# Two segments inverted as one pair at the start, and the feed-forward one step behind the chain from chunk 1 on

## The chip, the cores and the metric

One core of one Trainium2 chip runs the whole program. The metric is the device time of one execution in microseconds, median of several. The engines are TensorE (PE; PEld is its weight load), VectorE (DVE), ScalarE (ACT), GpSimd (POOL) and the queue of SyncE (SP) that issues most transfers.

## What is computed

A delta-rule attention, token by token, and a gated MLP on its output (batch 4, 8 heads, 768 tokens, head width 48; model width 384, 1024 hidden):

```python
for t in range(S):                       # k_n = k / (|k| + 1e-6)
    y[:, :, t] = q_t @ state
    v_old = k_n_t @ state
    state = state + beta_t * outer(k_n_t, v_t - v_old)
x = y as [B, S, 384]
h = gelu_tanh(x @ w_in); u, v = halves of h
v_n = layer_norm(v) * g_ln
out = x + (u * (w_sg @ v_n + b_sg)) @ w_out
```

## The kernel before

The recurrence runs in 12 chunks of 64 tokens; two chunks are a segment (six segments). Two batches lie side by side on the partitions, and 16 columns j hold heads and halves. For each chunk:

- `gram` makes k'k and k'q on TensorE and ScalarE copies them to GM (8 buffers). `kgram` makes k'k alone, `qgram` k'q alone; `dense` makes a whole gram without a chain beside it. The keys and queries come by `kload` (KD, two buffers, for grams) and `qload` (KQ, for the chain); `vload` and `tload` bring v and k by token.
- `gstore` writes the 32x32 diagonal blocks to DRAM (gd), four transfers a chunk; `zload` reads them back as lanes (tile zl), one 32x32 matrix per partition, one transfer a segment.
- `lanes` inverts them on VectorE: a copy of the diagonals (L323), two triangles cut by GpSimd (L325, `triu`), a reciprocal root (L176 to L184), scaling (L352), then for each row an outer product and an addition (L368, L375), and a last scaling (L396). It handles one segment (m = 1) or a pair (m = 2) in the same instructions. `zstore` writes the result to DRAM (zd, L421), `zfetch` reads it per chunk into Z and zk (L430, L435); `turned` transposes zk (L444), `corner_a` and `corner_b` build the off-diagonal block of the 64x64 inverse on TensorE.
- `above` masks k'q (L257), `vprep` scales v (L483).
- `chain` has the serial steps old0, own0, state0, old1, own1, state1: products with the state S, an addition into v on VectorE after old0 and old1 (L510, "the first and second addition"), copies by ScalarE (L532, L545, L560). A step of the chain is dealt alternately with a piece of a later chunk's gram.

The feed-forward of a chunk (`Ffn`) has a turn (transposes, L664, and the split into xh and xl, L665, L668), four `gate` groups and two `values` groups (L642 to L644, L678) with their gelu and moments (L684, L690). Its weights w_in come as 64-bit words and are decoded on VectorE in six pieces of three units each (`decode_win`, L584 to L602, ScalarE's copy at L594); the first three pieces serve the gates, the others the values. The load of piece k + 2 is issued on GpSimd's queue when piece k is done.

The order is written out by hand. Ahead of the loop stand the first inversion and grams; then the loop goes through `TURNS`, pairs (chunk of the chain, chunk of the feed-forward). Before, these are (0, none), (1, none), (2, none), (3, 0), (none, 1), (none, 2), (4, 3), (5, 4), ... (11, 10), (none, 11). A turn without a chain ends with a `zfetch` and both corners of the next chunk; `zfetch` for chunk 4 is issued twice. VectorE's background work (lanes, decoding) stands in the list `bg` with a cost for each unit; every step of a turn gives `tick` its planned cost times SHARE[turn] / length, and as many units are issued as the credit pays for. `lanes_done` and `until` issue the rest at once. All engines run their instructions in the order of issue.

Groups before: segments 0 and 1 alone, (2, 3) and (4, 5) as pairs. The lanes of (2, 3) are queued at the end of chunk 1's turn, together with their zload, those of (4, 5) in the turn before chunk 4.

From chunk 8 on (`c == NCH - 4`) the weights of the spatial part are brought in beside the turns; after the last turn comes the spatial part.

Of the kernel before, what the change touches and what calls it, by code (L numbers as in the profile page):

```python
# [26 lines left out]
NP = 16  # L27
# [13 lines left out]
N_GRAMS = 6  # L41
N_EARLY = 5
N_ROWS = (0, 6, 1)
N_COLS = (0, 5, 1)
GROUPS = ((0,), (1,), (2, 3), (4, 5))
# [3 lines left out]
TURNS = ((0, None), (1, None), (2, None), (3, 0), (None, 1), (None, 2),  # L49
         *((c, c - 1) for c in range(4, NCH)), (None, NCH - 1))  # L50
TURNED = {0: 0, 1: 1, 3: 2, 4: 3, **{c + 2: c for c in range(4, NCH)}}
# [3 lines left out]
def delta_rule_gmlp_kernel(  # L55
# [134 lines left out]
    gdt, zsrc, ztile, zds, zks, ns, nvs, ztks, j1s = {}, {}, {}, {}, {}, {}, {}, {}, {}  # L190
# [22 lines left out]
    def kgram(c):  # L213
        def phase(e):
            st = {}

            def step(h):
                if h == 0:
                    st["ps"] = bank().rearrange("p (j t) -> p j t", t=T)
                for sd in range(2):  # L220
                    kk = KD[c % N_2][OWN[sd], 0, 8 * e + h]
                    mm(st["ps"][TOK[sd ^ e], h], kk, kk)

            def done():
                nc.scalar.copy(out=GM[c % N_M][:, 8 * e:8 * e + 8, 0], in_=st["ps"])

            return step, done

        return phase(0), phase(1)
# [79 lines left out]
    def lanes(g):  # L309
# [56 lines left out]
        def outer(i, r0, r1, at):  # L366
            w = 31 - i
            tv.tensor_tensor(  # L368
                out=st["tmp"][:, at:at + m * (r1 - r0) * w].rearrange("p (m r t) -> p m r t", m=m, t=w),
                in0=z[:, :, r0:r1, i:i + 1].broadcast_to([P, m, r1 - r0, w]),  # L370
                in1=z[:, :, i:i + 1, i + 1:32].broadcast_to([P, m, r1 - r0, w]), op=ALU.mult)

        def add(i, r0, r1, at):
            w = 31 - i
            tv.tensor_tensor(  # L375
                out=z[:, :, r0:r1, i + 1:32], in0=z[:, :, r0:r1, i + 1:32],
                in1=st["tmp"][:, at:at + m * (r1 - r0) * w].rearrange("p (m r t) -> p m r t", m=m, t=w),
                op=ALU.add)

        us = lambda n: (0.13 if m == 1 else 0.17) + n / 960  # L380
        ops = [(f, us(32 * m)) for f in first] + [(scale, m * us(1024))]
        for i in range(1, 31):
            w = 31 - i
            if i <= N_ROWS[m]:
                ops += [(lambda a=a, r=r, i=i: row(a, r, i), us(w)) for r in range(i) for a in range(m)]
            elif w <= N_COLS[m]:
                ops += [(lambda a=a, t=t, i=i: column(a, t, i), us(i)) for t in range(i + 1, 32) for a in range(m)]
            else:
                parts = [(0, i // 2, 0), (i // 2, i, 256)] if m == 1 else [(0, i, 0)]
                ops += [(lambda i=i, p=p, f=f: f(i, *p), us(m * (p[1] - p[0]) * w)) for f in (outer, add) for p in parts]  # L390
# [3 lines left out]
        def last():  # L394
            for a in range(m):
                tv.tensor_tensor(  # L396
                    out=z[:, a], in0=z[:, a], in1=nb[:, a].unsqueeze(1).broadcast_to([P, 32, 32]), op=ALU.mult)
            ztile[g] = z

        return ops + [(lambda: tv.memset(dg, 1.0), us(0)), (last, m * us(1024)), (lambda: zstore(g), 0.0)]  # L400
# [15 lines left out]
    def zstore(g):  # L416

        z = ztile[g]
        for a, s in enumerate(GROUPS[g]):
            zd = dram.tile([2, 2, 2, NP, 32, 32], F32, name="zd", bufs=4)  # L420
            nc.sync.dma_start(out=zd.rearrange("a b c j s t -> (a b c j) s t"), in_=z[:, a])  # L421
            zds[s] = zd
# [383 lines left out]
    for c, q in ((0, nc.sync), (1, nc.scalar)):  # L806
        load(q, KD[c][:, 0], kqT[c, 0:2])
# [9 lines left out]
    for c in range(2):  # L817
# [5 lines left out]
    zload(0)  # L823
    for _ in range(N_EARLY):
# [8 lines left out]
    kload(2)  # L833
    kload(3)
    vload(0)
    tload(0)
    qload(0)
    for c in (2, 3):
        dense(c)
        gstore(c, (nc.sync,))  # L840
    zload(1)
    qload(1)
    kload(4)
    kload(5)
    for op, _ in first:
        op()
    norms(0)
    for c in range(2):
        q0, q1 = qgram(c)
        deal([q0], [q1])  # L850
    zfetch(0, nc.scalar)
    zfetch(1, nc.sync)
    bg += lanes(1) + win
    above(0)
    vprep(0)
    tick(5.0)
    for c in (4, 5):
        dense(c)
    kload(6)
    win_load(2, nc.sync)  # L860
    for c in (4, 5):
        gstore(c, (nc.sync,))
# [4 lines left out]
    tick(6.0)  # L867
# [18 lines left out]
    SHARE = (20.0, 20.0, 19.0, 20.0, 16.0, 16.0, 13.0, 13.0, 13.0, 13.0, 11.0, 11.0)  # L886
    units, turns = [], {}
    ffn = None
    for at, (c, f) in enumerate(TURNS):
# [55 lines left out]
        kload(new + 1)  # L945
        does("old0")
        if n is not None and n // 2 in zds and n not in zks:
            zfetch(n, nc.sync)
        if n is not None:
            above(n)  # L950
        if f == 0:
            until(lambda: not win_left)
# [5 lines left out]
        if c:  # L958
            qload(c + 1)
        feeds("values", 4)  # L960
        does("old1")
        unit()
        feeds("values", 4)
        does("own1")
        if c is not None:
# [19 lines left out]

        if ch:
# [5 lines left out]
        if at in TURNED:  # L992
            turns[TURNED[at]] = following = Ffn(TURNED[at])
# [20 lines left out]
        if c == 1:  # L1014
            zload(2)
            zload(3)
            bg.extend(lanes(2))
        if n == 4:
            zload(4)
            zload(5)  # L1020
            bg.extend(lanes(3))
# [123 lines left out]
```

## Time and profile before

| what | us |
|---|---|
| runs | 541.64, 538.8, 541.56 |
| median | 541.56 |
| span of the profiled execution | 538.2 |
| TensorE busy | 441.4 (82%) |
| VectorE busy | 346.6 (64%) |
| ScalarE busy | 171.8 (32%) |
| GpSimd busy | 74.9 (14%) |

The page gives the profiled execution's span, not the time around it; the median of the runs lies 3.4 us above the span. The chain of work that ended last is 61% TensorE, 17% VectorE and 7% transfers. Shares of the whole span mix stages with different limits, so the rows below are read by stretches: about 0 to 62 us is the front, 62 to 284 the turns of chunks 0 to 7, 284 to 370 the turns of chunks 8 to 11, the rest the spatial part.

### The profile page before, as it was taken

To read this page: it belongs to the slowest core of one execution; us is meant where nothing else is said; L and a number is where in the kernel's file an instruction comes from. 1 tells how busy PE (TensorE), PEld (TensorE's weight loads), DVE (VectorE), ACT (ScalarE), POOL (GpSimd) and SP (SyncE) were. 2 spreads that over 40 slices of the span, in tenths; PEclk is the share of its full clock that TensorE was granted. 3 is DMA by queue.
4 is the path that set the end of the run, shared out by engine and by line. 5 is a ranking of instruction groups with operands and counts; after the bars stand their busy time and mean duration, and the time that the engine had idled before them with its cause. 6 is when DMAs were issued, how large, how long until landed. Compare 5 with 4: busy or idle time off the path is not lost.

```text
span 538.2 us, 17698 instructions
## 1 busy us (share of the span) xinstructions
PE 441.4 (82%) x7691; PEld 395.2 (73%) x7691; DVE 346.6 (64%) x858; ACT 171.8 (32%) x383; POOL 74.9 (14%) x87
## 2 busy tenths in 40 slices
PE   4316785570889949898989896999998999999997
PEld 2316475470778748687777775878898999999997
DVE  3999999648997229689913359643599636623332
ACT  3222333230423522333533533444534213211110
POOL 2100002102201004010010110000024223222130
PEclk9555756555599969899999998899999999999999
DMA  7987858965538796645955868265857753344204
GB/s 181 278 199 195 179 156 211 248 174 126 156 95 237 218 206 165 195 117 165 314 146 155 277 154 250 65 202 163 246 161 187 214 166 104 103 147 147 74 16 132
DMA packets 111965, 93.18 MB, mean 173 GB/s; under 512 B 74768, under 2 KB 88016, under 8 KB 111888
## 3 DMA queue, kind: packets, MB, share of 16 engines
q1 hardware_dynamic: 101504, 68.23, 45.3%
q0 software_dynamic: 6032, 22.28, 15.0%
q10 hardware_dynamic: 4352, 1.54, 1.2%
q8 instruction: 60, 0.98, 0.8%
q14 instruction: 17, 0.14, 0.1%
HBM read 63.69 MB, written 28.34 MB: 171 GB/s over the span
## 4 chain that ended last, share of the span: by engine, by line
PE 61%; DVE 17%; DMA 7%; issue 7%; ACT 4%; SPq 4%; ACTq 1%; DVEq 0%
PE ps L81 19%; PE ps L642 12%; PE ps L644 11%; PE ps L643 11%; PE ps L678 8%; DVE ztmp L368 3%; DVE zl L375 3%; DMA kd<-kqT 2%; DMA vraw<-vD 2%; PE ps L664 1%; DMA gd<-gm 1%; DMA zl<-gd 1%; SPq L752 1%; ACT gm L295 1%; DVE zl L357 1%
## 5 line engine op out<-in xcount | busy, mean ns | idle before, releaser
L81 PEld LDWEIGHTS ps<-s,kq 48*64 48x64 f32 x1408 | 55.8, 159 | 21.3 <-issue 14.8
L81 PE MATMUL ps<-s,kq 48*64 48x48 f32 x1408 | 63.1, 245 | 9.7 <-issue 8.3
L785 POOL TENSOR_TENSOR ga<-ga,uT 128x384 f32<-128x384 f32 x32 | 36.3, 1140 | 165.8 <-DVE ga L782 120.9
L81 PE MATMUL ps<-kd 48*64 48x128 f32 (+1 forms) x768 | 40.2, 337 | 19.4 <-DMA kd<-kqT 17.4
L81 PE MATMUL ps<-v,z 64*64 64x48 f32 x768 | 33.7, 244 | 23.2 <-DVE v L510 13.8
L81 PEld LDWEIGHTS ps<-kd 48*64 48x64 f32 x768 | 33.8, 177 | 22.9 <-DMA kd<-kqT 15.3
L81 PEld LDWEIGHTS ps<-v,z 64*64 64x64 f32 x768 | 30.4, 159 | 24.5 <-DVE v L510 14.4
L368 DVE TENSOR_TENSOR ztmp<-zl 128x120 f32<-128x120 f32 (+25 forms) x132 | 45.9, 372 | 2.2
L375 DVE TENSOR_TENSOR zl<-zl,ztmp 128x120 f32<-128x120 f32 (+25 forms) x132 | 45.7, 370 | 1.6
L642 PE MATMUL ps<-xh,winh 128*128 128x256 f32 x144 | 45.7, 317 | 0.9 <-DVE xl L668 0.9
L643 PE MATMUL ps<-xl,winh 128*128 128x256 f32 x144 | 42.1, 293 | 0.4 <-DVE xl L668 0.3
L644 PE MATMUL ps<-xh,winl 128*128 128x256 f32 x144 | 41.8, 290 | 0.0
L647 ACT CAST gh<-ga 128x384 fp32r<-128x384 f32 x32 | 16.3, 511 | 77.3 <-POOL ga L785 63.3
L81 PE MATMUL ps<-u,gm 64*64 64x48 f32 x768 | 34.1, 245 | 2.6 <-ACT u L532 1.9
L648 DVE TENSOR_TENSOR gl<-ga,gh 128x384 fp32r<-128x384 f32 x32 | 18.1, 565 | 26.8 <-ACT gh L647 26.7
L532 ACT COPY u<-ps 128x384 f32<-128x384 f32 x24 | 11.5, 479 | 70.6 <-PE ps L81 70.6
L644 PE MATMUL ps<-wouth,gl 128*128 128x384 f32 x96 | 32.3, 340 | 1.5 <-DVE gl L648 1.5
L81 PEld LDWEIGHTS ps<-u,gm 64*64 64x64 f32 x768 | 30.2, 159 | 4.4 <-ACT u L532 2.4
L642 PE MATMUL ps<-wsgh,vnh 128*128 128x384 f32 x96 | 32.7, 340 | 0.7 <-ACT vnh L755 0.6
L81 PE MATMUL ps<-u,kt 64*48 64x48 f32 x704 | 27.3, 234 | 6.4 <-issue 4.6
L643 PE MATMUL ps<-wsgl,winh 128*128 128x384 f32 x96 | 32.5, 339 | 0.0
L642 PE MATMUL ps<-wsgh,winh 128*128 128x384 f32 x96 | 32.5, 339 | 0.0
(127 smaller groups left out, 1097.2 us busy)
## 6 DMA issues: line engine op xcount, KB each, us to landing
kq<-kqT POOLq DMA_DIRECT2D x10, 896.0 KB, 6.8
uD<-ut SPq DMA_DIRECT2D x12, 512.0 KB, 5.2
vD<-vg SPq DMA_DIRECT2D x24, 256.0 KB, 4.0
vraw<-vD SPq DMA_DIRECT2D x48, 128.0 KB, 3.1
uT<-uD SPq DMA_DIRECT2D x8, 768.0 KB, 5.4
kd<-kqT SPq DMA_DIRECT2D x6, 896.0 KB, 8.3
xD<-x SPq DMA_DIRECT2D x12, 384.0 KB, 6.9
x<-xD SPq DMA_DIRECT2D x48, 96.0 KB, 2.8
```

The lines of the kernel that those rows point to most:

```text
L81: return nc.tensor.matmul(out=out, lhsT=lhsT, rhs=rhs, start=start, stop=stop, skip_group_check=True)
L295: nc.scalar.copy(out=GM[c % N_M][:, js], in_=st["ps"])
L368: tv.tensor_tensor(out=st["tmp"][:, at:at + m * (r1 - r0) * w].rearrange("p (m r t) -> p m r t", m=m, t=w), in0=z[:, :, r0:r1, i:i + 1].br ...
L375: tv.tensor_tensor(out=z[:, :, r0:r1, i + 1:32], in0=z[:, :, r0:r1, i + 1:32], in1=st["tmp"][:, at:at + m * (r1 - r0) * w].rearrange("p (m ...
L532: ins = mark(nc.scalar.copy(out=u[:, js[e]], in_=ub[e]))
L642: nc.tensor.matmul(out=ps, lhsT=sh, rhs=mh, start=(first and i == 0), stop=False)
L643: nc.tensor.matmul(out=ps, lhsT=sh, rhs=ml, start=False, stop=False)
L644: nc.tensor.matmul(out=ps, lhsT=sl, rhs=mh, start=False, stop=(last and i == n - 1))
L647: nc.scalar.copy(out=hi, in_=src)
L648: nc.vector.tensor_tensor(out=lo, in0=src, in1=hi.bitcast(F32), op=ALU.subtract)
L678: nc.tensor.matmul(out=self.ps, lhsT=(self.xl if k == 2 else self.xh)[:, cc, bi], rhs=(winl if k == 1 else winh)[:, cc, DH:], start=(i == ...
L785: nc.gpsimd.tensor_tensor(out=gv, in0=gv, in1=uT[:, :, d], op=ALU.mult)
```

## The change

Segments 0 and 1 are inverted as one pair. For that the key halves of chunks 0 to 3 are loaded first, ahead of the weights, on the queues of SP and ScalarE in turn; four `kgram`s follow, whose two copies are shared between VectorE and ScalarE; the queries of chunks 2 and 3 get a `qgram` of their own in turns 1 and 2, and `above` for these two follows it. Grams 4, 5 and 6 are made ahead of the loop beside the inversion, so every turn makes the gram of chunk turn + 7 instead of turn + 6. The feed-forward runs one chunk behind the chain from chunk 1 on; no turn but the last is without a chain. Six units of decoding, not five, stand ahead of the first inversion, and the other four pieces in turns 0 and 1. Each segment of a pair is stored as soon as its own last scaling is done; the first store goes by ScalarE's queue. The zloads of (2, 3) move to the end of turn 0 and their lanes to turn 1 behind the second addition; those of (4, 5) to the end of turn 4 and to turn 5 behind old0. SHARE is written anew. The split into two halves that single inversions used goes. The work from chunk 8 on is not touched.

```diff
-N_GRAMS = 6
-N_EARLY = 5
-N_ROWS = (0, 6, 1)
-N_COLS = (0, 5, 1)
-GROUPS = ((0,), (1,), (2, 3), (4, 5))
+N_GRAMS = 7
+N_EARLY = 6
+N_ROWS = 1
+N_COLS = 1
+GROUPS = ((0, 1), (2, 3), (4, 5))
-TURNS = ((0, None), (1, None), (2, None), (3, 0), (None, 1), (None, 2),
-         *((c, c - 1) for c in range(4, NCH)), (None, NCH - 1))
-TURNED = {0: 0, 1: 1, 3: 2, 4: 3, **{c + 2: c for c in range(4, NCH)}}
+TURNS = ((0, None), *((c, c - 1) for c in range(1, NCH)), (None, NCH - 1))
...
-                nc.scalar.copy(out=GM[c % N_M][:, 8 * e:8 * e + 8, 0], in_=st["ps"])
+                copy = nc.scalar.copy if e else nc.vector.tensor_copy
+                copy(out=GM[c % N_M][:, 8 * e:8 * e + 8, 0], in_=st["ps"])
...
-        def last():
-            for a in range(m):
-                tv.tensor_tensor(
-                    out=z[:, a], in0=z[:, a], in1=nb[:, a].unsqueeze(1).broadcast_to([P, 32, 32]), op=ALU.mult)
-            ztile[g] = z
+        def last(a):
+            tv.tensor_tensor(
+                out=z[:, a], in0=z[:, a], in1=nb[:, a].unsqueeze(1).broadcast_to([P, 32, 32]), op=ALU.mult)
+            zstore(ss[a], z[:, a])
...
-            nc.sync.dma_start(out=zd.rearrange("a b c j s t -> (a b c j) s t"), in_=z[:, a])
+        (nc.sync if s else nc.scalar).dma_start(out=zd.rearrange("a b c j s t -> (a b c j) s t"), in_=z)
...
-    for c, q in ((0, nc.sync), (1, nc.scalar)):
-        load(q, KD[c][:, 0], kqT[c, 0:2])
+    for c in range(4):
+        load((nc.sync, nc.scalar)[c % 2], KD[c % N_2][:, c // N_2], kqT[c, 0:2])
...
-    for c in range(2):
+    for c in range(4):
         k0, k1 = kgram(c)
         deal([k0], [k1])
         gstore(c, (nc.sync, nc.scalar))
...
     zload(0)
+    zload(1)
...
+    win_load(2, nc.sync)
+    qload(0)
+    kload(4)
     vload(0)
+    kload(5)
     tload(0)
-    qload(0)
-    for c in (2, 3):
-        dense(c)
-        gstore(c, (nc.sync,))
-    zload(1)
     qload(1)
-    kload(4)
-    kload(5)
-    for op, _ in first:
+    for op, _ in first[:20]:
         op()
     norms(0)
-    for c in range(2):
-        q0, q1 = qgram(c)
-        deal([q0], [q1])
+    for c in (0, 4, 5):
+        if c:
+            dense(c)
+            gstore(c, (nc.sync,))
+        else:
+            q0, q1 = qgram(c)
+            deal([q0], [q1])
+    kload(6)
+    q0, q1 = qgram(1)
+    deal([q0], [q1])
+    dense(6)
+    gstore(6, (nc.sync,))
+    kload(7)
+    for op, _ in first[20:]:
+        op()
+    bg += win
     zfetch(0, nc.scalar)
-    zfetch(1, nc.sync)
-    bg += lanes(1) + win
     above(0)
     vprep(0)
-    tick(5.0)
...
+    zfetch(1, nc.sync)
+    tick(2.5)
     keep_warm(bank(), N_KICK, kick)
...
-    SHARE = (20.0, 20.0, 19.0, 20.0, 16.0, 16.0, 13.0, 13.0, 13.0, 13.0, 11.0, 11.0)
+    SHARE = (16.0, 17.0, 18.0, 18.0, 13.0, 17.0, 17.0, 13.0, 11.0, 11.0, 11.0, 11.0)
...
-        kload(new + 1)
+        if at:
+            kload(new + 1)
         does("old0")
+        if c == 5:
+            bg.extend(lanes(2))
...
-        if n is not None:
+        if n is not None and n not in (2, 3):
             above(n)
         if f == 0:
-            until(lambda: not win_left)
+            until(lambda: min(win_left, default=NC) >= NC)
...
-        if c:
+        if c and c > 2:
             qload(c + 1)
+        if f == 0:
+            until(lambda: not win_left)
         feeds("values", 4)
         does("old1")
+        if c == 1:
+            bg.extend(lanes(1))
...
         does("own1")
+        if c in (0, 1):
+            qload(c + 2)
+        if not at:
+            kload(new + 1)
...
+        if n in (2, 3):
+            q0, q1 = qgram(n)
+            deal([q0], [q1])
+            above(n)
...
-        if c == 1:
+        if c == 0:
             zload(2)
             zload(3)
-            bg.extend(lanes(2))
-        if n == 4:
+        if c == 4:
             zload(4)
             zload(5)
-            bg.extend(lanes(3))
```

## Rows read from the trace of the kernel before

**Rows 1.** The cores: span and mean granted clock (1.0 is 2.4 GHz).

```profile
core 0: 538.2 us, clock 0.866
```

**Rows 2.** Stretches: length, busy PE, PEld, DVE, ACT, POOL, PEclk, DMA, GB/s.

```profile
0.00:10.00 10.00, 6.11 (x137) 3.12 (x137) 1.99 (x7) 2.36 (x3) 3.25 (x12) 1.00 0.67 207
130.00:140.00 10.00, 5.54 (x203) 5.22 (x206) 9.41 (x21) 1.71 (x4) 0.73 (x1) 0.50 0.36 105
143.20:165.30 22.10, 20.65 (x454) 17.75 (x444) 20.92 (x37) 8.61 (x18) 1.34 (x3) 0.88 0.54 155
188.80:195.60 6.80, 0.06 (x1) 0.00 (x0) 2.18 (x4) 1.16 (x5) 0.00 (x0) 0.81 0.85 175
198.40:224.10 25.70, 22.42 (x519) 18.57 (x508) 19.32 (x43) 9.03 (x22) 7.00 (x7) 0.84 0.74 196
224.10:243.30 19.20, 19.18 (x479) 16.06 (x478) 16.42 (x29) 7.83 (x21) 2.14 (x3) 1.00 0.51 124
243.30:262.70 19.40, 17.88 (x444) 14.70 (x443) 18.61 (x39) 8.00 (x19) 2.14 (x3) 1.00 0.68 197
284.10:304.40 20.30, 19.10 (x510) 15.96 (x509) 6.24 (x11) 8.20 (x20) 2.14 (x3) 1.00 0.61 171
```

**Rows 3.** TensorE in order of time: start, duration, line, operation, [idle before, releaser].

```profile
58.18 0.75 PE L81 MATMUL ps<-z,gm 32*32 32x32 f32 x64
...
61.73 0.76 PE L81 MATMUL ps<-kd 48*64 48x128 f32 x10 [1.58 <-DMA kd<-kqT]
...
80.40 0.26 PE L81 MATMUL ps<-s,kq 48*64 48x48 f32 x2
...
133.80 0.34 PE L81 MATMUL ps<-v,z 64*64 64x48 f32 x2 [12.14 <-DVE v L510]
...
195.67 1.29 PE L81 MATMUL ps<-z,gm 32*32 32x32 f32 x64 [6.81 <-DMA z<-zd]
```

**Rows 4.** VectorE and SP's queue in order of time, around the first pair (same columns).

```profile
100.59 0.43 DVE L584 TENSOR_SCALAR vg<-ut 128x512 int32<-128x512 int32 x1 [3.84 <-DMA ut<-w_in]
...
110.44 3.37 SPq L240 DMA_DIRECT2D gd<-gm  x4
...
122.92 0.22 DVE L323 COPY d<-zl 128x64 f32<-128x64 f32 x1 [8.58 <-DMA zl<-gd]
...
123.40 1.15 DVE L181 SCALAR_TENSOR_TENSOR rsq_t<-d,rsq_y 128x64 f32<-128x64 f32 x1
...
130.29 2.36 DVE L352 TENSOR_TENSOR zl<-zl,nb 128x1024 f32<-128x1024 f32 x2
...
169.20 2.33 DVE L396 TENSOR_TENSOR zl<-zl,nb 128x1024 f32<-128x1024 f32 x2
```

**Rows 5.** The front, in order of time: decoding, first inversion, its store and fetch.

```profile
8.77 0.43 DVE L584 TENSOR_SCALAR vg<-ut 128x512 int32<-128x512 int32 x1 [6.96 <-DMA ut<-w_in]
...
18.72 1.25 DVE L176 TENSOR_SCALAR rsq_y<-d 128x32 int32<-128x32 int32 x1
...
47.17 0.35 SPq L421 DMA_DIRECT2D zd<-zl  x1
...
49.77 0.68 SPq L430 DMA_DIRECT2D zk<-zd  x1
```

**Rows 6.** Instructions on the tile zl alone, stretches of a single and a pair.

```profile
18.00:47.20 29.20, 23.26 (x116) 0.24 (x1) 1.56 (x1) 0.56 0.90 246
...
122.90:171.60 48.70, 34.99 (x66) 0.00 (x0) 2.49 (x2) 0.74 0.55 151
```

**Rows 7.** In order of time: an addition, a fetch of z, a corner.

```profile
155.87 0.55 DVE L510 TENSOR_TENSOR v<-v,ps 128x384 f32<-128x384 f32 x1
...
191.00 1.29 SPq L430 DMA_DIRECT2D zk<-zd  x2
...
299.57 0.75 PE L81 MATMUL ps<-z,gm 32*32 32x32 f32 x64
```

## What the change was predicted to do

> **What bounds the kernel now.** I read the span first, then the busy time by stretch, then the waits in front of TensorE's instructions, then VectorE in order of time. The profiled execution spans 538.2 us [rows 1]; the median of the runs, 541.56, is 3.4 above that, and I take this rest as fixed. I write T(c) for the start of chunk c's turn on TensorE.
>
> The stretches [rows 2] show three parts. From T(8) at 284.1 to the end (254.1 us) the chunk turns, the decoding of the last weights and the spatial part run with TensorE nearly full at its upper clock; the diff changes nothing there. From T(5) to T(9) four turns take 80.3 us, 20.1 each, and the reader sees TensorE full at clock 1.00 while VectorE is anywhere between 6 and 19 us busy: TensorE sets this pace. Before that VectorE is 9.4 of 10 us busy and the clock is down at 0.50 (1.2 GHz): the inversions on VectorE set the pace. So a new order can gain only ahead of T(8), and its worth is how far T(8) moves.
>
> Three holes ahead of T(8) are what the change could close [rows 3]: TensorE waits 12.14 us for one addition on VectorE, which stands behind the copy that waits 8.58 us for the pair's tile [rows 4]; it waits 6.81 us for z of chunk 4; and the feed-forwards of chunks 1 and 2 have two turns of their own (165.3 to 188.7, without a chain beside them).
>
> **The front: the pair comes later.** Before, VectorE decodes five units of weights from 8.77 and starts the inversion of segment 0 at 18.72 [rows 5], 2.0 a unit; the single's instructions on its tile take 23.26 us [rows 6], and the result is stored at 47.17. After, two more key loads (0.92 MB) go ahead of the weights. At the 207 GB/s of the first 10 us [rows 2] that is 4.4 us if nothing overlaps, and nothing if they overlap wholly; I take 3.5, since the queues are already filled from the first microsecond. With six units, 8.8 + 3.5 + 6 x 2.0 = 24.3 for the start. The other road, stores and loads of four chunks instead of two, adds one more chunk pair's stores, some 3.4 us as in [rows 4], to the 18.72 of [rows 5]; it ends near 22.1 and is hidden. TensorE's copies of the grams are now shared by VectorE; they run before weights land and cost nothing, or 1.3 us if they don't (two of about 0.65 each, estimated from a multiply of twice the columns at 2.33 for two [rows 4]).
>
> A pair takes 35.0 us on its tile [rows 6] and about 6 for the reciprocal root ahead of the scaling (122.92 to 130.29 less the copy and one mask multiply of 1.2 [rows 4]; the first of them took 1.15, beside GpSimd's selects, where the copy ahead of it took 0.22). Segment 0 is stored one multiply (1.2) before the end: 24.3 + 6 + 35 - 1.2 = 64.1. Store to fetch is 2.6 (47.17 to 49.77 [rows 5]), fetch to corner 4.7 (191.00 to 195.67 [rows 3, 7]): corner_a of chunk 0 at 71.4, and T(0) 3.5 later, 74.9, as 58.18 to 61.73 in [rows 3]. That is **13.2 us later** than before; bounds 10 and 17.
>
> **Turn 0** has no feed-forward and takes 61.73 to 80.40, 18.7 [rows 3]: T(1) = 93.6. The four weight pieces left lie beside it on VectorE, about 6 us each (three units of 2.0). But the loads of pieces 4 and 5 are started only when 2 and 3 are done, and behind a piece that isn't there stands chunk 1's first addition; the row of before shows such a wait at 3.84 us [rows 4]. I add 4, with 0 and 8 as ends (8: also the keys of chunk 8, which are now queued on SP behind a query load).
>
> **Chunks 1 to 3** now carry the feed-forward of the chunk before, so the two turns without a chain and the double fetch of z for chunk 4 are gone. Against TensorE's pace, 22.1 us for a turn with a gram (143.2 to 165.3 [rows 2]), stands VectorE. The pair (2, 3) is queued in turn 1 after the second addition and wanted at the end of turn 3. The planner's costs of one pair sum to 39.65 (16 x 0.237 + 2.47 + 0.80 + 29.94 + 0.17 + 2.47); the measured 41 is 1.04 of that. SHARE and the planned lengths hand out 10.9 in the rest of turn 1, 19.0 in turn 2 and the 8.6 that are left ahead of segment 2's store in turn 3. Beside it each turn has 6.2 us of its own VectorE work (the turn from 284.1 [rows 2]). The second addition of a chunk comes 12.6 after its turn's start (143.2 to 155.87 [rows 2, 7]): 93.6 + 4 + 12.6 = 110.2. Then VectorE is never idle: 16.3 (11.3 + 5 left of the turn), 25.9 (19.7 + 6.2), 11.1 (8.9 + 2.2), sum 53.3: segment 2 is ready at 163.5, and with 7.3 of store and fetch corner_a of chunk 4 starts at 170.8. TensorE alone would be there near 160: the next thing late is z of chunk 4. The queries of chunks 2 and 3, now a gram of their own, add some 1 us of TensorE to turns 1 and 2, under VectorE's cover; they'd cost 2 us if the cover is gone. The mask multiply waits behind them, on VectorE's queue, with lanes work behind it; below zero is excluded, since it is the same multiply, later.
>
> **Chunk 4 to 8.** From corner_a to the next turn is 4.8 (299.57 to 304.4 [rows 2, 7]), and some 1.1 more with half a gram in it (half of the 2.0 by which the turn from 143.2 is longer than 20.1). After a wait of such length TensorE is slow: between 188.8 and 195.6 the granted clock fell to 0.81, and the corner then took 1.29 instead of 0.75 [rows 2, 3, 7]. I add 2 for the steps behind it (0 to 4). T(4) = 178.7, against 198.4: **19.7 sooner**. A gram turn follows: T(5) = 200.8.
> The Trainium skill ("TensorE: Matmul & The Clock Gate", section "Why this matters for your kernels") tells one to leave no long pause between bursts of matmuls, or the engine falls back to its lower clock; this trace agrees, 6.81 us of waiting and 0.81. By it the change, which trades many short holes for one at the corner, pays the 2 us; without it the sum would be 2 us lower.
>
> The last pair can be loaded only after gram 11, which is now made in turn 4. From the store of grams to the copy of the diagonals were 12.5 us (110.44 to 122.92 [rows 4]), and the store starts about 1 us before T(5). I take the copy at T(5) + 10 (8 to 12): 210.8. Some 16 small instructions, 6 us, stand between it and the chunk's second addition, so TensorE loses about 5 us in turn 5, as it lost 12.14 in turn 2 of before. From there VectorE is full again: turn 5 22.3 (17.1 x 1.04 + 4.5), turn 6 24.8 (17.9 x 1.04 + 6.2), turn 7 5.1 to the store of segment 4: 263.0; corner_a of chunk 8 at 270.3; T(8) = **275.1**, against 284.1. The share of 17 in turns 5 and 6, where before had 13, gives most of the gain of T(4) back: these turns took 19.2 and 19.4 [rows 2].
>
> **The sum.** 284.1 - 275.1 = 9.0 us sooner; what follows is unchanged: span 529.2, time 541.56 - 9.0 = 532.6. The terms in T(8): front +13.2, turns 0 to 3 with the two lone feed-forwards -32.9, chunks 4 to 7 +10.7. With the lower ends of front, load wait, clock and copy together (-3, -4, -2, -2) 521.6, with the upper ones 544.
>
> **The rivals.**
> (a) VectorE is hidden, TensorE sets the pace. For it: before's turn 6 had VectorE 18.6 of 19.4 us busy and no longer turn. Then chunk 4's corner is at 160.6 (93.6 + 4 + two turns of 23.7 + 15.5), 10 sooner: 522; with the last pair hidden too (T(5) + 3 x 20.1, another 14 sooner) 508. Against it: the additions stand in one queue with the lanes, and 25.9 us of work don't fit in 23.7. Chance of one of them 0.17, of both 0.04.
> (b) Slower: VectorE stands still at the copy of a pair's diagonals, with the chunk's addition behind it. Place: turns 1 and 5, where the pairs are queued; price: each microsecond that the tile lands late moves T(8) by one. At 9 us of extra lateness in sum the gain is gone; with the row's 8.58 us of standing [rows 4] in each of both turns, 17.2, the time is 550. For it: SP's queue has four stores, two loads that wait for them, and fetches, in strict order. Against it: in turn 1 the loads start a dozen microseconds ahead of the copy. Chance 0.12.
> (c) The change doesn't do what it says: the step of lag is taken out, but both corners (chunk 4 and 8) wait for their z 4 us longer each, because 512 KB stores and the fetches share the queues with the query loads, which now come in the same turns: 532.6 + 8 = 540.6, no change. Chance 0.15.
>
> **How the numbers follow.** The forecast, 0.52, is 532.6. What a measurement of this kernel can tell from no change is about 0.5%, 2.7 us. Faster: forecast nearly whole (0.50) and (a) 0.21, together 0.71; within: (c) and the forecast's upper edge, 0.17; slower 0.12. The range reaches from (a) with one leg to the upper ends of the sum, 520 to 544; left out are (a) with both legs and a piece of the other (0.09) and the greater part of (b) (0.08).
>
> **What would show it.** Right: first inversion on VectorE near 24 and its first store near 64; T(0) near 75; VectorE without idle from some 110 to 163; a wait of TensorE for z ahead of corner_a of chunk 4, T(4) near 179; an idle VectorE from there to a copy that waits for its tile near 211; turns 5 and 6 of 25 us and more; from T(8) on the same 254 us. Wrong: turns 2, 3 and 6 at 20 to 23 us with VectorE waiting for TensorE (a), a copy that waits over 8 us in turn 1 (b), or a front over 80.

## The result and the profile after

The changed kernel takes 546.39 us (median of five runs, 544.88 to 554.9) where the kernel before takes 541.56: the ratio, 1.0115 with a 95% interval of 1.0074 to 1.0155, says **about 6 us slower** (the two medians lie 4.8 apart). The forecast was 532.6 in a range that ended at 544. Executions of one kernel spread by some 2% here (544.88 to 554.9 for this one), so a time below is a median, while a trace shows one execution: e_front's (541.19) is the shortest of its run, e_half1's (545.89) and e_all's (542.58) are the longest of theirs.

The profiled execution took 548.37. Its core and its stretches by turn, from T(0) on, with the columns of [rows 2] (turn 3 is cut at 184.6, where the corner of chunk 4 starts):

```profile
core 0: 546.7 us, clock 0.862
82.00:103.10 21.10, 17.08 (x458) 15.00 (x454) 14.31 (x25) 9.37 (x20) 2.76 (x4) 0.50 0.64 180
103.10:131.10 28.00, 25.07 (x646) 20.64 (x637) 19.57 (x42) 14.41 (x34) 6.19 (x8) 0.87 0.85 253
131.10:157.30 26.20, 25.04 (x637) 21.30 (x636) 22.56 (x42) 11.54 (x27) 2.87 (x4) 0.82 0.52 133
157.30:184.60 27.30, 16.28 (x398) 13.89 (x399) 17.89 (x35) 6.32 (x17) 2.14 (x3) 0.81 0.76 194
184.60:195.10 10.50, 10.48 (x176) 7.71 (x176) 1.99 (x4) 4.46 (x10) 0.00 (x0) 0.51 0.53 175
195.10:214.80 19.70, 19.70 (x573) 16.48 (x572) 6.12 (x11) 9.85 (x22) 0.71 (x1) 1.00 0.46 124
214.80:243.00 28.20, 20.55 (x474) 17.51 (x473) 19.94 (x45) 7.25 (x20) 6.04 (x7) 0.88 0.76 205
243.00:266.50 23.50, 20.15 (x465) 16.86 (x451) 22.67 (x40) 9.09 (x22) 2.16 (x3) 0.93 0.52 149
266.50:290.50 24.00, 20.97 (x511) 17.46 (x511) 16.20 (x43) 8.72 (x24) 2.16 (x3) 0.93 0.58 161
```

Chunk 4's turn starts at 195.1 against 198.4, chunk 5's at 214.8 against 224.1: there the change is 9.3 us ahead. The three turns that follow take 75.7 where [rows 2] and the start of chunk 8's turn at 284.1 give 60.0 before, and T(8) comes at 290.5, 6.4 late; the rest, 256.2 against 254.1, adds 2, though its code is the same (in the traces below this rest runs from 250.8 in e_keys to 259.9 in e_all). TensorE, in order of time (start, duration, line, operation, [idle before, releaser]), as in [rows 3]:

```profile
62.08 0.49 PE L79 MATMUL ps<-kd 48*64 48x128 f32 x4 [7.31 <-DMA kd<-kqT]
...
79.41 1.07 PE L79 MATMUL ps<-z,gm 32*32 32x32 f32 x64 [7.76 <-DMA z<-zd]
...
184.57 0.63 PE L79 MATMUL ps<-z,gm 32*32 32x32 f32 x10 [8.41 <-DMA z<-zd]
...
231.27 0.35 PE L79 MATMUL ps<-v,z 64*64 64x48 f32 x2 [5.65 <-DVE v L506]
...
285.53 0.66 PE L79 MATMUL ps<-z,gm 32*32 32x32 f32 x32 [0.68 <-DMA z<-zd]
...
293.98 0.34 PE L79 MATMUL ps<-s,kq 48*64 48x48 f32 x2 [2.48 <-issue]
```

The 12.14 us wait for an addition [rows 3] is gone, and so are the two turns of feed-forward alone. In their place stand waits of 7.76 and 8.41 us for z ahead of the corners of chunks 0 and 4, and 5.65 for the second addition of turn 5. The front, VectorE and GpSimd's select first, then ScalarE and the two queues (compare [rows 5]):

```profile
15.26 0.69 DVE L224 COPY gm<-ps 128x512 f32<-128x512 f32 x1 [3.33 <-PE ps L79]
15.87 0.42 DVE L580 TENSOR_SCALAR vg<-ut 128x512 int32<-128x512 int32 x1
...
19.30 0.69 DVE L594 TENSOR_TENSOR ut<-ut,vg 128x512 f32<-128x512 f32 x1
...
24.63 2.91 POOL L324 TENSOR_SCALAR_AFFINE_SELECT zl<-zl 128x1024 f32<-128x1024 f32 x2 [2.12 <-ACT d L322]
24.67 1.75 DVE L594 TENSOR_TENSOR ut<-ut,vg 128x512 f32<-128x512 f32 x1
26.34 1.73 DVE L597 TENSOR_TENSOR vg<-vg,winh 128x512 f32<-128x512 f32 x1
...
28.71 0.19 DVE L174 TENSOR_SCALAR rsq_y<-d 128x64 int32<-128x64 int32 x1
```

```profile
64.09 1.07 ACT L294 COPY gm<-ps 128x512 f32<-128x512 f32 x2 [8.22 <-PE ps L79]
65.80 1.07 ACT L294 COPY gm<-ps 128x512 f32<-128x512 f32 x2 [0.63 <-PE ps L79]
68.75 0.34 ACTq L417 DMA_DIRECT2D zd<-zl  x1
...
56.14 0.44 SPq L134 DMA_DIRECT2D kd<-kqT  x1
66.90 1.90 SPq L239 DMA_DIRECT2D gd<-gm  x4
68.89 0.44 SPq L134 DMA_DIRECT2D kd<-kqT  x1
69.88 0.34 SPq L417 DMA_DIRECT2D zd<-zl  x1
```

The decode starts at 15.87, behind VectorE's own gram copy, and the pair's root at 28.71. Segment 0 goes out at 68.75 on ScalarE's queue, 1.9 us behind the copies of gram 6, whose keys TensorE waited 7.31 us for; the keys of chunk 7 go ahead of the store of segment 1.

### The profile page after: what moved, and what is told of

It is laid out like the page before. It is cut to its first block, busy times and chain, and to the rows that moved or that the text cites. A ratio compares the mean times of both kernels' runs of the same rounds, so it can differ in the third digit from the quotient of the medians.

```text
span 546.7 us, 17768 instructions
## 1 busy us (share of the span) xinstructions
PE 450.4 (82%) x7819; PEld 399.1 (73%) x7819; DVE 335.7 (61%) x681; ACT 171.6 (31%) x379; POOL 72.8 (13%) x85
## 4 chain that ended last, share of the span: by engine, by line
PE 58%; DVE 21%; DMA 9%; issue 7%; ACT 3%; SPq 1%; DVEq 0%; ACTq 0%
PE ps L79 19%; PE ps L638 11%; PE ps L640 10%; PE ps L639 10%; PE ps L674 7%; DVE zl L378 5%; DVE ztmp L371 5%; DMA vraw<-vD 2%; DMA z<-zd 2%; DMA zd<-zl 2%; DMA zk<-zd 1%; PE ps L660 1%; DMA zl<-gd 1%; DMA kd<-kqT 1%; DVE vraw L753 1%
## 5 line engine op out<-in xcount | busy, mean ns | idle before, releaser
L79 PEld LDWEIGHTS ps<-s,kq 48*64 48x64 f32 x1408 | 53.3, 152 | 21.1 <-issue 13.4
L638 PE MATMUL ps<-xh,winh 128*128 128x256 f32 x144 | 49.2, 341 | 0.0
L371 DVE TENSOR_TENSOR ztmp<-zl 128x116 f32<-128x116 f32 (+13 forms) x84 | 43.7, 521 | 2.4
L378 DVE TENSOR_TENSOR zl<-zl,ztmp 128x116 f32<-128x116 f32 (+13 forms) x84 | 43.7, 520 | 2.5
L639 PE MATMUL ps<-xl,winh 128*128 128x256 f32 x144 | 44.5, 309 | 0.1
L640 PE MATMUL ps<-xh,winl 128*128 128x256 f32 x144 | 44.3, 308 | 0.0
L686 DVE BATCH_NORM_STATS2 bs<-vg 128x6 f32<-128x512 f32 x24 | 16.6, 690 | 28.0 <-ACT vg L680 27.9
L79 PE MATMUL ps<-u,gm 64*64 64x48 f32 x768 | 31.9, 239 | 1.9 <-issue 1.2
L638 PEld LDWEIGHTS ps<-xh,winh 128*128 128x128 f32 x144 | 30.6, 213 | 3.1 <-DVE vg L581 0.3
L640 PE MATMUL ps<-wsgh,winl 128*128 128x384 f32 x96 | 32.5, 339 | 0.0
```

Of the source, the lines that this page charges most:

```text
L79: return nc.tensor.matmul(out=out, lhsT=lhsT, rhs=rhs, start=start, stop=stop, skip_group_check=True)
L371: tv.tensor_tensor(out=products(i), in0=z[:, :, 0:i, i:i + 1].broadcast_to([P, m, i, w]), in1=z[:, :, i:i + 1, i + 1:32].broadcast_to([P, ...
L378: tv.tensor_tensor(out=at, in0=at, in1=products(i), op=ALU.add)
L638: nc.tensor.matmul(out=ps, lhsT=sh, rhs=mh, start=(first and i == 0), stop=False)
L639: nc.tensor.matmul(out=ps, lhsT=sh, rhs=ml, start=False, stop=False)
L640: nc.tensor.matmul(out=ps, lhsT=sl, rhs=mh, start=False, stop=(last and i == n - 1))
```

## The experiments

All ran with the kernel before beside them on the same chip. The ratio is to that kernel; the changed kernel stands at 1.0115, and an interval is about 0.4% to either side, so two runs have to lie some 0.6% apart to be told apart.

| run | what differs from the changed kernel | median us | ratio | 95% interval |
|---|---|---|---|---|
| e_half0 | first pair: rows 1 to 15 of 30 | 545.97 | 1.0077 | 1.0036 to 1.0119 |
| e_half1 | second pair: the same | 540.19 | 0.9997 | 0.9954 to 1.0041 |
| e_half2 | last pair: the same | 541.61 | 1.0058 | 1.0022 to 1.0093 |
| e_keys | keys of chunks 6, 7 sooner | 546.57 | 1.0135 | 1.0085 to 1.0185 |
| e_front | e_keys, two decode steps fewer ahead | 547.18 | 1.0078 | 1.0036 to 1.0120 |
| e_late | last pair queued later | 547.39 | 1.0120 | 1.0083 to 1.0157 |
| e_split | segments 4 and 5 alone | 540.0 | 0.9985 | 0.9955 to 1.0016 |
| e_warm | TensorE kept busy ahead of chunk 4 | 546.98 | 1.0136 | 1.0098 to 1.0173 |
| e_all | e_front and e_split | 534.55 | 0.9856 | 0.9819 to 0.9893 |
| e_best1 | e_front, segments 2 to 5 alone | 530.1 | 0.9828 | 0.9786 to 0.9869 |
| e_single | e_front, segments 0 and 1 alone | 579.34 | 1.0728 | 1.0680 to 1.0777 |
| e_best2 | e_best1, segments 0 and 1 alone | 563.67 | 1.0450 | 1.0399 to 1.0501 |

**Half of one pair's elimination.** In each run one pair stops after row 15; nothing else is left out. The first pair:

```diff
-        for i in range(1, 31):
+        for i in range(1, 16 if g == 0 else 31):
-            if g == 0 and i == 28:
+            if g == 0 and i == 13:
```

> The changed kernel with the elimination of the first pair (segments 0 and 1) stopped after row 15 of 30; about half of the row operations of that pair on VectorE, some 15 us, are left out, so the inverses of these two segments are not whole. VectorE theory (the end is set by a chain of three pairs on VectorE with their stores and fetches): turn 0 starts some 15 us sooner and all of it reaches the end, 546.4 - 15 = 531 (528 to 535). Rival (TensorE's or the queues' work in the front sets turn 0): grams 5 and 6 end near 66 us in the front, so turn 0 starts at most 5 us sooner and the time stays above 540.

The rival is right. Less work on VectorE hardly brought the front forward; chunk 0's corner starts at 76.40 (79.41 in the changed kernel), and the time, 0.4% lower, isn't told apart. TensorE of this run, in order of time:

```profile
60.47 0.49 PE L79 MATMUL ps<-kd 48*64 48x128 f32 x4 [7.53 <-DMA kd<-kqT]
...
76.40 0.28 PE L79 MATMUL ps<-z,gm 32*32 32x32 f32 x2 [8.23 <-DMA z<-zd]
```

The keys of chunk 6 come nearly as late as before (62.08 there), and gram 6's copies stand ahead of the store on ScalarE's queue: VectorE starts the last scaling at 51.54, and segment 0 is stored at 64.31. From there to the corner are 12.1 us. The front has two limits nearly level.

The second pair (the same line with `g == 1`):

> The changed kernel with the elimination of the second pair (segments 2 and 3) stopped after row 15; some 15 us of VectorE's work in turns 1 to 3 are left out. VectorE theory: the wait of 8.4 us for z ahead of chunk 4's corner goes, and turns 2 and 3 run at TensorE's pace: chunk 4's turn starts 12 to 16 us sooner, 546.4 - 14 = 532 (529 to 536). Rival (TensorE sets turns 1 to 3, only the fetch is late): 3 to 6 us sooner, 541 to 543.

Close to the rival: 1.2% less, not 2.6%. TensorE waits for no z at chunk 4's corner, and still the way there from T(1) takes 75.70 us (e_best1 below gives the same). The stretch in this run, columns as in [rows 2]:

```profile
105.00:180.70 75.70, 66.06 (x1674) 54.65 (x1670) 44.31 (x85) 31.29 (x71) 11.18 (x15) 0.88 0.71 201
```

The prediction had TensorE alone there in 67 us, 160.6 less 93.6. In the changed kernel it is 81.4, so the pair on VectorE was the bound, but by 6 us only.

The last pair (`g == 2`):

> The changed kernel with the elimination of the third pair (segments 4 and 5) stopped after row 15; some 15 us of VectorE's work in turns 5 to 7 are left out. VectorE theory: turns 6 and 7 run at TensorE's pace of 20.1, chunk 8's turn starts 8 to 12 us sooner, 546.4 - 10 = 536 (533 to 540); the wait for the copy in turn 5 stays. Rival (the wait for the copy in turn 5 alone is what these turns lose): no change, 545 to 548.

Between the two: segments 4 and 5 are stored near 255 instead of 276, chunk 8's corner waits for nothing and starts at 281.49 instead of 285.53; the wait for the addition in turn 5 stays, 6.76.

**The front's two limits.** First the keys alone, then with the decode:

```diff
-N_EARLY = 6
+N_EARLY = 4          # e_front only
...
         if c:
             dense(c)
+            kload(c + 2)
             gstore(c, (nc.sync,))
...
-    kload(6)
...
-    kload(7)
```

> The changed kernel with the key loads of chunks 6 and 7 issued right behind the grams that free their buffers, ahead of the stores of grams 4 and 5, so that chunk 7's keys (896 KB) no longer run beside the store and fetch of the first pair. Contention theory (the 10.7 us from the store of segment 0 to the corner, where before had 7.3 in its rows, come from that transfer): 7.5 to 8.5 us instead, the end 2 to 3 us sooner, 543.5. Rival (the second store of the pair or the queue's own order makes it long): within 1 us of 546.4.

> The changed kernel with both limits of its front moved: the keys of chunks 6 and 7 are loaded ahead of the gram stores of chunks 4 and 5, and four instead of six steps of the decode stand ahead of the first pair (so about 4 us of decode move behind it). All of the computation is done. With two limits nearly level (VectorE's store of segment 0 at 68.7, the second half of gram 6's copies at 66.9 ahead of it on ScalarE's queue) neither alone showed at the end; with both moved the root should start near 24.5, segment 0 be stored near 64.5, its corner start near 72 and chunk 0's turn near 74.5 (now 82.0). If the front is passed on, the time is 537 to 541. Rival: what follows is set by waits that don't move with chunk 0's turn (the transfer of the inverses of chunks 4 and 8); then the corner of chunk 4 still starts within 3 us of 184.6 or the gain goes at chunk 8, and the time is 544 to 548.

In e_keys segment 0 is stored at 68.62 as before, but its corner starts 7.3 us later instead of 10.7, with no keys in flight beside it. The stretch from the store of segment 0 to chunk 0's corner, as stretches with the columns of [rows 2], first e_keys:

```profile
68.60:75.90 7.30, 2.92 (x7) 0.78 (x6) 6.60 (x9) 0.00 (x0) 0.00 (x0) 0.73 0.85 214
```

then the changed kernel, with the same way at chunk 4 and chunk 8 (the last two columns are the busy share of the transfer engines and GB/s):

```profile
68.70:79.40 10.70, 2.95 (x7) 0.78 (x6) 6.11 (x10) 0.00 (x0) 0.00 (x0) 0.66 1.00 240
173.40:184.60 11.20, 2.79 (x78) 2.36 (x77) 2.48 (x3) 2.21 (x8) 1.54 (x3) 0.70 1.04 242
276.20:285.50 9.30, 8.65 (x195) 7.07 (x193) 3.70 (x15) 3.28 (x10) 2.16 (x3) 0.96 0.71 205
```

The two longest ways run with the transfer engines full; the third, 9.3 us at a share of 0.71, isn't explained by that. At chunk 4 it is the queries and v of a later chunk that go out on GpSimd's queue beside the store of segment 2 on SP's:

```profile
172.79 0.72 POOL L134 DMA_DIRECT2D v<-vtok  x1 [16.13 <-PE ps L79]
173.51 0.72 POOL L134 DMA_DIRECT2D kq<-kqT  x1
173.37 0.34 SPq L417 DMA_DIRECT2D zd<-zl  x1
```

No run moved these, so for chunk 4 the cause is argued from the full engines, and for chunk 8 it is open. At the end of e_keys nothing is left of the 3.5 us. Its chunk 8's corner still starts 3.8 sooner than in the changed kernel, at 281.77; the trace loses them right behind that, where a later part of chunk 8's z is late:

```profile
288.64 0.39 PE L79 MATMUL ps<-z,gm 32*32 32x32 f32 x12 [6.66 <-DMA z<-zd]
```

In e_front segment 0 is stored at 67.37 (expected 64.5), since the root waits for the diagonals; ScalarE's copy of them, VectorE's root, and TensorE at T(8):

```profile
25.06 0.30 ACT L322 COPY d<-zl 128x64 f32<-128x64 f32 x1 [5.68 <-DMA zl<-gd]
25.40 0.20 DVE L174 TENSOR_SCALAR rsq_y<-d 128x64 int32<-128x64 int32 x1 [2.31 <-ACT d L322]
...
285.43 0.38 PE L79 MATMUL ps<-s,kq 48*64 48x48 f32 x6
```

Chunk 0's corner starts at 74.47, 4.9 sooner, chunk 4's 3.3 sooner, at 181.26, and T(8) 5.1 sooner: in this execution the last pair passes the gain of the front on. The time of the run is the rival's, 547.18, and its ratio lies 0.4% below the changed kernel's, which these intervals tell neither from nothing nor from those 5 us. Whether the front alone pays stays open.

**The last pair.** Queued later:

```diff
         does("old0")
-        if c == 5:
-            bg.extend(lanes(2))
...
         does("old1")
+        if c == 5:
+            bg.extend(lanes(2))
```

> The changed kernel with the last pair queued behind the second addition of turn 5 in place of ahead of the first. All of the computation is done. If the in-order stall sets the end (VectorE stands at the copy of the pair's diagonals, which waits for its transfer, while the addition that TensorE waits 5.65 us for stands behind it), that wait goes and the time falls by 4 to 6 us, to about 541. If the pair's own length from its copy to the store of segment 4 (51.7 us) sets chunk 8's turn, the stall only changes places: the copy comes at the same time or up to 3 us later, chunk 8's turn starts at 290 to 293 and the time is 545 to 549.

The stall only changes places: turn 5 loses its wait, and the corner of chunk 8 waits 10.58 us for z, at 288.49 instead of 285.53 (T(8) at 296.26, past the 290 to 293 expected); the time stays. TensorE of this run, in order of time:

```profile
288.49 0.28 PE L79 MATMUL ps<-z,gm 32*32 32x32 f32 x2 [10.58 <-DMA z<-zd]
```

Taken apart, which lets segment 4 begin a turn sooner, since it needs gram 9 and not gram 11:

```diff
-GROUPS = ((0, 1), (2, 3), (4, 5))
+GROUPS = ((0, 1), (2, 3), (4,), (5,))
-        if c == 5:
-            bg.extend(lanes(2))
+        if c == 6:
+            bg.extend(lanes(3))
-        if c == 1:
-            bg.extend(lanes(1))
+        if c in (1, 4):
+            bg.extend(lanes({1: 1, 4: 2}[c]))
-        if c == 4:
-            zload(4)
-            zload(5)
+        if c in (3, 4):
+            zload(c + 1)
...
-    SHARE = (16.0, 17.0, 18.0, 18.0, 13.0, 17.0, 17.0, 13.0, 11.0, 11.0, 11.0, 11.0)
+    SHARE = (16.0, 17.0, 18.0, 18.0, 15.0, 17.0, 17.0, 17.0, 11.0, 11.0, 11.0, 11.0)
```

> The changed kernel with its last pair taken apart: segment 4 alone is loaded after turn 3 and begins in turn 4, segment 5 alone begins in turn 6 (groups 0+1, 2+3, 4, 5). All of the computation is done. In the changed kernel the last pair begins at 224.5, behind the gram of chunk 11, stores segment 4 at 276.2, and chunk 8's turn starts at 290.5, 75.7 us after chunk 5's; in the kernel before the same three turns took 60.0. If VectorE's late pair is what stretches them, segment 4 (some 31 us of work and 14 us of the turns' own, from about 203) is stored near 248, the corner of chunk 8 waits for nothing, the waits of 5.65 and 3.35 us for the addition in turns 5 and 6 go or shrink, chunk 8's turn starts 9 to 14 us sooner and the time is about 535 (532 to 538). Rival: the turns of TensorE take that long by themselves at the granted clock and VectorE's wait is hidden in them; then chunk 8's turn starts within 3 us of 290 and the time stays at 543 to 548.

Some 1.3%, 7 us: the whole loss to the kernel before, if less than the 532 to 538 expected. T(8) comes 8.0 sooner, not 9 to 14, and in turn 6 a wait of 3.46 for the addition stays. The new SHARE of turns 4 and 7 was not tried by itself. Segment 4 is stored at 238.35 instead of 276.19, and chunk 8's corner starts with no wait ahead of it; SP's queue and TensorE of this run:

```profile
238.35 0.34 SPq L417 DMA_DIRECT2D zd<-zl  x1
...
277.71 0.49 PE L79 MATMUL ps<-z,gm 32*32 32x32 f32 x34
```

From chunk 5's corner to chunk 8's it is 70.5 us (76.7 in the changed kernel, 64.2 before): half of the lengthening was the late pair.

**The clock in a filled wait.**

```diff
             ready()
+            if n == 4:
+                keep_warm(bank(), 36, busy[:, 0:P])
             corner("corner_a")
```

> The changed kernel with 36 matmuls of zeros (128x512, about 0.21 us each at full clock) ahead of the corner of chunk 4, where TensorE waits 8.41 us for the inverse's transfer. Nothing of the computation is left out. In the changed kernel the clock granted in that wait falls to half, and the 10.5 us from the corner to chunk 4's turn run at 0.51. If the wait costs that too, the clock stays at full through the filled wait, the corner still starts within 1 us of 11 us behind the store of segment 2, and the stretch to chunk 4's turn takes 7 to 8 us; in the total 2 to 4 us, about what five rounds can tell. Rival: the stretch is slow from its own waits (copies, evictions) and not from the clock; then it stays at 10 to 11 us.

The wait ahead of the corner and the stretch behind it up to T(4); as stretches with the same columns; first the changed kernel (its second stretch stands above, 10.50 us at 0.51):

```profile
176.00:184.60 8.60, 0.19 (x3) 0.06 (x2) 1.40 (x2) 0.96 (x5) 0.00 (x0) 0.61 1.19 287
```

then e_warm:

```profile
173.90:183.80 9.90, 7.92 (x37) 3.46 (x37) 1.32 (x2) 0.96 (x5) 0.00 (x0) 1.00 1.05 216
183.80:191.40 7.60, 7.58 (x176) 5.79 (x176) 1.98 (x5) 3.87 (x9) 0.00 (x0) 0.78 0.61 218
```

The same 176 matmuls take 2.9 us less, so the corner's wait cost that on top of itself. The corner came 12.9 us behind the store of segment 2 and not 11, still with 1.95 of waiting for z, so the filling didn't hold it up. The end doesn't show the gain: T(4) is 3.7 sooner, turn 5's wait grows from 5.65 to 6.61, chunk 8's corner is still 4.4 sooner (281.13), but from there to T(8) this execution takes 9.0 us instead of 5.0, 3.13 of them in a hole for which the profile shows no cause:

```profile
281.13:290.15 9.02, 5.89 (x145) 4.25 (x144) 2.98 (x6) 4.14 (x13) 0.00 (x0) 0.80 0.98 291
```

**Together.**

> The front of the run e_front and the last two single segments of the run e_split together. All of the computation is done. If the front and the last pair are two separate losses, their gains add: about 7 us sooner at chunk 0's turn, 9 to 14 us less between the turns of chunks 5 and 8, 526 to 533 in all, below the kernel before. If TensorE's own pace is the bound once VectorE is out of the way, the second gain eats the first: 534 to 540.

1.3% below e_split and 2.2% below e_front, and faster than the kernel before by 1.4%: with the last pair taken apart the front is worth some 7 us. The time, 534.55, is 1.5 above what was expected and just inside the rival's range, but a second gain that eats the first would not lie 2.2% below e_front. Together the two gain 2.6%, against 1.7% for their sum. That difference, 0.9%, is hardly more than the intervals leave open, so it isn't shown that the late pair hid the front's gain; e_front's trace speaks against it.

In e_best1 segments 2 and 3 are taken apart as well (`GROUPS = ((0, 1), (2,), (3,), (4,), (5,))`, 2 and 3 queued in turn 1, 4 in turn 4, 5 in turn 6; the tile of lanes is kept and refilled by halves, segment 5 is loaded after turn 5, and SHARE is written anew):

> The front of the run e_front, and every segment from 2 on inverted alone (groups 0+1, 2, 3, 4, 5): segments 2 and 3 are queued one behind the other in turn 1, segment 4 in turn 4, segment 5 in turn 6. All of the computation is done. It asks what the pair in the middle costs by coming in just at its corner: in the run e_all the corner of chunk 4 still waited 7.98 us, and the clock fell in that wait. Segment 2 alone is some 31 us of work and 14 of the turns' own from about 110, stored near 158, so chunk 4's corner should wait for nothing: 8 to 11 us sooner at chunk 4's turn, 523 to 530 in all. If TensorE's turns then take what the run e_half1 showed (75.7 us from chunk 1's turn to chunk 4's corner, with no wait there), the corner comes at 96.3 + 75.7 = 172, again 8 to 10 sooner. Rival: two single segments cost VectorE 16 us more than a pair in turns 1 to 4, the additions that TensorE waits for come later by as much as is won, and segment 3 now comes in just at the corner of chunk 6: 532 to 540.

Chunk 4's corner starts at 174.14 with nothing to wait for, 75.85 us behind T(1) at 98.29; chunk 8's at 268.45. TensorE of this run, in order of time, where a wait would stand in brackets:

```profile
174.14 0.45 PE L79 MATMUL ps<-z,gm 32*32 32x32 f32 x31
...
268.45 0.44 PE L79 MATMUL ps<-z,gm 32*32 32x32 f32 x30
```

At 530.1 us, 1.7% below the kernel before and at the upper edge of what was expected, it is the lowest here, though its VectorE is busy for 356.3 us and that of the changed kernel for 335.7. It lies 0.3% below e_all, too little to be told apart: the trace shows the wait at chunk 4's corner gone, the time doesn't show what that is worth.

**The headline undone.** Segments 0 and 1 one by one, segment 1 behind the decode (`bg += win + lanes(1)`, zload of 2 and 3 at the end of turn 1):

> The run e_front with the headline part of the change undone: segments 0 and 1 are inverted one by one, segment 1 behind the decode of the first layer's weights; the pair of segments 2 and 3 is then loaded and queued at the end of turn 1 (groups 0, 1, 2+3, 4+5). All of the computation is done. If the pair pays for itself, because it takes some 40 us of VectorE where two singles take some 59: segment 0 is stored near 54 instead of 67.4 and chunk 0's turn starts 9 to 12 us sooner, but segment 1 comes in near 115 and holds chunk 2's turn at 126 to 132 (129.9 in e_front), the pair of 2 and 3 is copied near 120 instead of 112, and the corner of chunk 4 comes 4 to 8 us later than e_front's 181.3: the time is 2 to 7 us above e_front's, 547 to 552. Rival: an earlier chunk 0 gives TensorE work ahead that it keeps, as it does in the kernel before, and the time is 536 to 543.

> The run e_best1 with the pair of segments 0 and 1 undone too, so that every segment is inverted alone (segment 1 behind the decode). All of the computation is done. Here segment 2 is not late, so what the pair costs or gives shows without the corner of chunk 4 behind it: chunk 0's turn should start 9 to 12 us sooner than e_best1's (corner at 74.1), chunk 1's by as much, and chunk 2's wait for segment 1, stored near 115, at 124 to 130 (128.0 in e_best1). If the pair at the front was a net gain, the time is 530 to 536; if an earlier start carries through turns 0 and 1 and segment 1 comes in before it is wanted, 520 to 527.

The pair pays, as expected, but far more than expected: these runs are 6.5% and 6.3% slower than their twins with the pair, where 1% was forecast. Chunk 0's corner does come 10 to 12 us sooner (64.26 and 62.12), but chunk 2's then waits for segment 1. TensorE of e_single, in order of time:

```profile
139.04 0.28 PE L79 MATMUL ps<-z,gm 32*32 32x32 f32 x2 [23.63 <-DMA z<-zd]
```

That corner comes 17.8 later than e_front's (121.25). Chunk 4's then waits 15.93 us for z of the pair behind segment 1 and comes 35.5 later (216.71), which is most of the loss. Segment 1 begins at 102.9 and is stored at 132.2, not near 115: VectorE's decode steps stand in one queue with its waits for the fetch of chunk 0 (7.7) and for TensorE's products ahead of an addition (5.4). So with the feed-forward one step behind, this order of singles is no way out. An order with segment 1 ahead of the decode, as the kernel before has it, was not tried here, nor was SHARE fitted to the new order, so what the pair itself is worth against the best order of singles stays open.

## Why the prediction was wrong

The frame held: the waits appeared where they were named (z at chunk 4's corner, the copy of the last pair behind an idle VectorE, the addition in turn 5), and VectorE's work was sized well. The sum failed in its other terms:

| step of the prediction | said | measured |
|---|---|---|
| front: segment 0 stored | 64.1 | 68.75 |
| store to corner of chunk 0 | 7.3 | 10.7 |
| corner to T(0) | 3.5 | 2.6 |
| T(0) to T(1) | 18.7 | 21.1 |
| T(1) to store of segment 2 | 69.9 | 70.3 |
| store to corner of chunk 4 | 7.3 | 11.2 |
| corner to T(4) | 7.9 | 10.5 |
| T(4) to T(5) | 22.1 | 19.7 |
| T(5) to the copy of the last pair | 10 | 9.7 |
| copy to store of segment 4 | 52.2 | 51.7 |
| store to corner of chunk 8 | 7.3 | 9.3 |
| corner to T(8) | 4.8 | 5.0 |

**The front** was 7.1 us late at T(0). 4.4 of it are its start: the step that failed is "they run before weights land and cost nothing". The weights were there by 12.1 (the second piece was issued at 1.79 and landed 10.3 us later), close to the 12.3 reckoned, but the decode stands behind VectorE's new copy of chunk 3's gram, which waits for TensorE until 15.26; and two of its last steps, beside GpSimd's selects, took 1.75 and 1.73 instead of 0.69. Most of the rest is the fetch of z. The second limit, the keys of chunk 6 that e_half0 brought out, wasn't in the prediction at all. Nor was the road of the diagonals hidden: reckoned to end near 22.1, it set the start in e_front, at 25.40, so without the late decode the start would still have been 1 us behind 24.3.

**Store to corner**, 7.3 three times, was the largest term that failed. It was put together from two stretches of the kernel before (2.6 and 4.7) in which less was moving:

```profile
47.17:49.77 2.60, 2.14 (x44) 1.77 (x38) 2.53 (x5) 0.00 (x0) 0.46 (x1) 0.50 0.52 208
191.00:195.67 4.67, 0.00 (x1) 0.03 (x1) 0.62 (x2) 0.00 (x0) 0.00 (x0) 0.72 0.79 152
```

It measured 10.7, 11.2 and 9.3, in sum 9.3 too little. Rival (c) named such a delay, with a chance of 0.15: 5.9 of its 8 us came at its two corners, and 3.4 at one that it doesn't name. That other transfers are the cause is shown for chunk 0: the way takes 10.7 with full transfer engines beside it and 7.3 without the keys (e_keys). At chunk 4 it fits, and at chunk 8 it is open.

**Turns 0 to 3.** Turn 0 was 2.4 longer than its row: TensorE is busy 1.5 more in it and stands 1.49 for nothing that the profile shows. From T(1) to the store of segment 2 the sum was right within 0.4, by two misses that cancel: the load wait of 4 was 1.31 and held nothing up, and the 53.3 us without idle were 57.5 (115.85 to 173.37), 51.3 of them busy, so VectorE did stand idle, for 6.2. TensorE's pace was far off: 67 us reckoned up to chunk 4's corner, 75.7 and 75.85 where it waits for no z (e_half1, e_best1; busy for 66.06 of them in e_half1). At that pace rival (a) couldn't give its 522.

**The clock** behind chunk 4's corner: mechanism right, size 2 where 4.6 came, since the wait was longer and all 10.5 us ran at 0.51. e_warm took 2.9 of it back.

**The last pair.** Its terms were right to 0.5 us: the loss of the last three turns was forecast, and taken as the price of a good start. e_split, without it, is 1.3% faster. Turn 4 ahead of it was 2.4 shorter than reckoned, the one large miss to the good. The slower rival (b), an in-order stall, was there with 5.65 us in turn 5, but e_late shows that it isn't what sets the end.

The misses add up to 15.4 us at T(8). Behind it the profiled execution loses 2.1 more, and the 3.4 between its span and the time, taken as fixed, were 1.7 (548.37 against 546.7): 15.8 in all, 548.37 against 532.6. The median of the runs misses by 13.8.

## What to carry to other kernels

When a change takes out slack, price what then comes just in time with the latency of the row with the fullest transfer engines, not the emptiest. Follow a gain at the start through the trace up to the last place where something comes just in time: the gains of e_keys and e_warm were whole at chunk 8's corner and gone 14 and 9 us behind it. One execution isn't the run: e_front's trace is 6 us shorter than its median. Batching two inversions saves engine time (335.7 us of VectorE against 356.3) and costs lead time (segment 4 stored 38 us later than alone): taking the last pair apart won 1.3%, taking the first one apart, in the one order tried, lost some 6%.

## What the runs showed of the hardware

Behind a hole of 2.48 us without work, ahead of 293.98, the granted clock was 0.50 (1.2 GHz) for some six microseconds. Stretches of the changed kernel ahead of it, behind it and later:

```profile
286.00:292.00 6.00, 5.50 (x163) 4.24 (x149) 3.41 (x7) 3.89 (x9) 0.00 (x0) 1.00 1.05 260
294.00:300.00 6.00, 6.00 (x84) 5.59 (x85) 1.69 (x2) 0.86 (x2) 0.00 (x0) 0.50 0.57 118
302.00:308.00 6.00, 6.00 (x147) 4.84 (x149) 1.78 (x3) 1.65 (x4) 1.33 (x2) 1.00 0.02 4
```

TensorE was busy for 21.86 us from that corner to the next (285.53 to 309.87) and for 18.99 in the same turn of the kernel before: 2.9 us of lower clock beside the 2.48 of the hole itself, though the profile shows no wait for data there. The other holes of over 2 us in the turns for which it shows no wait were followed by 0.50 too: 2.22 ahead of 128.55 (0.50 from 130.2 to 140.2), 2.34 ahead of 162.74 (164.3 to 167.5), 2.15 ahead of 271.72 (273.5 to 276.8). The Trainium skill ("TensorE: Matmul & The Clock Gate", section "Why this matters for your kernels") says to leave no long idle gaps between bursts of matmuls; these rows agree, and here 2.48 us were long enough. What TensorE waited for in such holes (1.49 ahead of 101.52, 2.48 here) no run here shows.
